# Taps summed by accumulating transposes, and the first layer's sums of two blocks split from their PSUM banks

## The chip, the cores and the metric

One core of a Trainium2 chip runs the kernel. The metric is the device time of one execution in microseconds (us), median of several runs. The profile comes from one execution of its own; its span is the part between its first and its last recorded instruction.

## The reference

```python
# attention: x is (2, 4096, 192); weight_gen is (2, 4096, 8 heads, 7 taps)
w = softmax(weight_gen over the 7 taps)
out[b, s, h, g] = sum over k of w[b, s, h, k] * x_pad[b, s + k, h, g]     # causal window of 7
# two dense layers over the 8192 tokens, d_model 192, d_ff 2048
h = x @ w_in1;  x = (h * cos(h)) @ w_out1
h = x @ w_in2;  return maximum(0.01 * h, h) @ w_out2
```

The kernel gets the four weight matrices as 64-bit floats, seen as pairs of 32-bit integers.

## The kernel before

**Blocks and chunks.** The 8192 tokens are 16 blocks of 512 (four groups of 128), taken in the order `LINE` = 2, 3, 0, 1, 4, 5, ... A block passes through attention, layer 0 and layer 1. A layer runs over 16 chunks of 128 hidden units. `hidden` (L707) makes one chunk's `h` (128 x 512) in a PSUM bank with five matmuls. After it ACT makes the turns of the angle `g` (L719), DVE the angle (L726), ACT the sine (L731), DVE the product (L736), and the result is split into `hi` and `lo` (a rounded part and the remainder, fp32r). Two projections add it up over the chunks in two banks `accm` and `accr`: `project_hi` with three matmuls (L763 to L765) and `project_lo` with two (L768, L769). So a chunk costs ten matmuls of 512 columns.

**192 = 128 + 64.** Of the 192 features, 128 are the main part (`tm`, `x0hi`, `x0lo`, `ihi`, `ilo`, `am`), 64 the rest (`tr`, `x0rh`, `x0rl`, `r`, `ar`). The rest's `hi` and `lo` weights are stacked on the 128 partitions of `r` by four DMAs (L661) from `whi` and `wlo`. So the fourth matmul of a chunk waits for those DMAs.

**Attention.** For blocks 2 and 3 (`SUMMED`), DVE multiplies each tap (L503, 128 x 768, three row buffers `pr`), and PE adds the seven taps up in the banks `tm` and `tr` by matmuls against the identity, which transposes as well (L508). The other 14 blocks add the taps on DVE and transpose once (L474, L479). The banks are then split: `x0hi` (ACT), `x0lo` (DVE), `x0rh` and `x0rl`.

**Weights.** Each layer's weights come in four groups, and each of these as an `in` and an `out` part. Loads into two `raw` buffers are followed by: size (ACT, L611), clamp (POOL, L614), shift (DVE, L619), merge (DVE, L625), low (ACT, L633), add (POOL, L638), then the split into hi (ACT) and lo (POOL). A `raw` buffer is free after merge and low. Only group (0, 0) is treated in two parts (main 512 columns, rest 256).

**Hand-over.** `take` copies a block's layer-0 sums out of the two banks (`om`, `sw`, `s`) and splits them into layer 1's `x1hi`, `x1lo`, `x1rh`, `x1rl`, the rest in halves (`place`).

**Order.** Nothing runs in a loop on the chip. A planner (`Plan.emit`) takes operations with due times and cost estimates and writes them out one by one; each engine, and the DMA queue SP, then works strictly in the order written. A `due` that changes, or a cost that changes, may move any later row. Names such as `pr_3_189` are tap 3 with a running number; `h_2_4` is chunk 4 of block 2.

Of the kernel before, what the change touches and what calls it, by code (L numbers as in the profile page):

```python
# [9 lines left out]
F32 = mybir.dt.float32  # L10
# [184 lines left out]
def conv_attention_moe_moe(ctx, tc, x, weight_gen, w_in1, w_out1, w_in2, w_out2, out):  # L195
# [68 lines left out]
    def minus(e, out, a, b):  # L264
        eng[e].tensor_tensor(out=out, in0=a, in1=b.bitcast(F32), op=ALU.subtract)  # L265
# [45 lines left out]
    def steps_of(t):  # L311
        return t()[:, : 2 * Q * CW].rearrange("p (s h k) -> p s h k", h=H, k=K)

    def softmax(s0, s1, due):
        n = s1 - s0
        w = temp([P, 16, H, K], "smw", 2, f"smw{s0}")
        m = temp([P, 16, H], "smm", 2, f"smm{s0}")
        k = ("smw", s0)
        part = n / 16
        early = s0 // Q in SUMMED  # L320
# [18 lines left out]
        op(due - 3, {"ACT": 0.2 + 0.8 * part + (2.6 if s0 // Q not in SUMMED else 0)}, lambda e: nc.scalar.activation(  # L339
            out=W(), in_=W(), func=AF.Exp), [k], [k], bufs)  # L340
# [15 lines left out]
    def x_load(b, due):  # L356
        t = Buf(lambda: xin.tile([P, (Q + HALO) * D], F32, tag="xt", name=f"xt{b}"), "xt", 2, line="xt")
        first = Q * b - HALO
        own = max(-first, 0)
        xt_of[b] = t, own  # L360

        def body(e, j0, j1):
            nc.sync.dma_start(out=t()[:, j0 * D : j1 * D], in_=xf[:, (first + j0) * D : (first + j1) * D])

        steps = [(HALO, Q + HALO), (own, HALO)] if b in SUMMED else [(own, Q + HALO)]
# [119 lines left out]
    def attention_summed(b, begins):  # L485

        xt, own = xt_of[b]
        ksm, smw, s0 = sm_of[b]
        tm, tr = bank(f"tm{b}", ("tq", 2)), bank(f"tr{b}", ("tq", 2))
        x_tiles(0, b)  # L490
        last = begins - 2
        for i, k in enumerate(reversed(range(K))):
            pr = row(f"pr{b}_{k}")
            reads = [ksm, ("xt", b, 1)]
            if k < HALO:
                reads.append(("xt", b, 2))
            if k < own:
                reads += [("xt", b, 0, *j) for j in ((0,), (1,), ("z", 0), ("z", 1))]

            def product(e, k=k, pr=pr):  # L500
                win = xt().rearrange("p (q h g) -> p q h g", h=H, g=G)[:, k : k + Q]
                wgt = steps_of(smw)[:, s0 : s0 + Q][:, :, :, k].unsqueeze(3).to_broadcast([P, Q, H, G])
                eng[e].tensor_tensor(out=pr().rearrange("p q (h g) -> p q h g", h=H), in0=win, in1=wgt, op=ALU.mult)  # L503

            def total(e, to, c, i=i, pr=pr):
                for q in range(Q):
                    v = pr()[:, q, c]
                    nc.tensor.matmul(  # L508
                        to()[: v.shape[-1], q * P : (q + 1) * P], v, ident,
                        start=i == 0 and q == 0, stop=i == K - 1 and q == Q - 1,  # L510
                    )

            due = last - (K - i) * PACE[b]
            op(due, {"DVE": 1.0}, product, reads, [("pr", b, k)], [xt, smw, pr])
            for to, key, c, late in ((tm, "tm", slice(0, P), 0.5), (tr, "tr", slice(P, D), 0.55)):
                op(due + late, {"PE": 0.58}, lambda e, to=to, c=c, total=total: total(e, to, c),
                   [("pr", b, k), "ident"] + ([(key, b)] if i else []), [(key, b)], [pr, to])
        turned(b, last, tm, tr)

# [37 lines left out]
    def weights(m, g):  # L557
# [9 lines left out]
        def load(raw):  # L567
            nc.sync.dma_start(out=raw()[:, : GF * P].rearrange("p c w -> p (c w)"), in_=wi[:P, c2])
# [10 lines left out]
            )  # L579

        U = 3 * half
        for i in ("in", "out"):
            due = need[m, g * GF] + {"in": -0.6, "out": 1.8}[i]
            raw = temp([P, U, 2], "raw", 2, f"w{n}{i}", I32)
# [1 line left out]
            v = temp([P, U], "wn", 2, f"wn{n}{i}", I32)  # L586
            if i == "in":
                parts = [(0, GF * P), (GF * P, U)]
                op(due - 6, {"SP": 1.75}, lambda e, raw=raw: load(raw), (), [("raw", n, i, 0)], [raw])
                for j in range(2):  # L590
                    op(due - 6, {"SP": 0.4}, lambda e, raw=raw, j=j: load_rest(raw, j), (), [("raw", n, i, 1, j)], [raw])
                loaded = [[("raw", n, i, 0)], [("raw", n, i, 1, 0), ("raw", n, i, 1, 1)]]
# [100 lines left out]
    def chunk(pos, st, m, b, f):  # L693
# [177 lines left out]
```

## Time and profile before

| | |
|---|---|
| three runs, median (lowest to highest) | 1248.27 us (1247.76 to 1248.58) |
| the profiled execution's own time | 1247.06 us |
| its span | 1245.2 us |
| PE busy | 1222.1 us |
| DVE, ACT, POOL busy | 890.6, 850.6, 448.0 us |

An engine's busy time is the time covered by its records. PE's matmuls overlap in the records (one of 512 columns is recorded as 0.39 us, but the next starts 0.23 us later), so for PE the distance from start to start counts.

### The profile page before, as it was taken

How to read it: one execution, taken by the hardware profiler on the slowest of the kernel's cores; microseconds unless marked ns; L12 is line 12 of the kernel's file. 1: busy time of each engine (PE TensorE's matmuls, PEld its weight loads, DVE VectorE, ACT ScalarE, POOL GpSimd, SP SyncE). 2: the span in 40 equal slices, each digit the busy share in tenths (PEclk: the TensorE clock that was granted, in tenths of full speed). 3: DMA queues.
4: the chain of work that ended last, by engine and by line, in shares of the span. 5: the costliest groups of instructions: out<-in, count | busy, mean ns of one | idle time of the engine just before them, and what ended most of it. 6: DMA issues, size and time to landing. Idle time of an engine off the chain costs nothing.

```text
span 1245.2 us, 15437 instructions
## 1 busy us (share of the span) xinstructions
PE 1222.1 (98%) x5524; PEld 1002.6 (81%) x5524; DVE 890.6 (72%) x1364; ACT 850.6 (68%) x1552; POOL 448.0 (36%) x340
## 2 busy tenths in 40 slices
PE   7999899999999999999999999999999999999998
PEld 6777687788888888888888888888888888888886
DVE  6799899889676777757677686777768676655433
ACT  4798766788675777667676767767667576655654
POOL 3686632566232323323233233323324232322000
PEclk9999999999999999999999999999999999999999
DMA  5343410100001010010101001010000100000000
GB/s 181 91 127 93 132 41 13 45 33 1 1 1 60 1 45 1 1 45 1 46 1 60 1 1 45 1 45 1 25 21 1 46 1 13 1 1 13 1 13 26
DMA packets 15469, 39.51 MB, mean 32 GB/s; under 512 B 1828, under 2 KB 8482, under 8 KB 15392
## 3 DMA queue, kind: packets, MB, share of 16 engines
q1 hardware_dynamic: 15392, 38.53, 9.6%
q8 instruction: 43, 0.70, 0.2%
q14 instruction: 34, 0.28, 0.1%
HBM read 30.13 MB, written 6.29 MB: 29 GB/s over the span
## 4 chain that ended last, share of the span: by engine, by line
PE 91%; DVE 4%; ACT 2%; DMA 1%; issue 1%; SPq 0%; POOL 0%; DVEq 0%; ACTq 0%; POOLq 0%
PE h L707 44%; PE acc0r L768 4%; PE acc0m L763 4%; PE acc1m L763 4%; PE acc1r L768 4%; PE acc1m L769 4%; PE acc1r L765 4%; PE acc1m L764 4%; PE acc0r L765 4%; PE acc0m L769 4%; PE acc0m L764 4%; PE tm L508 1%; PE tr L508 1%; DVE g L726 1%; PE pm L809 1%
## 5 line engine op out<-in xcount | busy, mean ns | idle before, releaser
L265 POOL TENSOR_TENSOR lo<-g,hi 128x512 fp32r<-128x512 f32 x240 | 340.1, 1418 | 606.3 <-ACT hi L260 497.0
L726 DVE SCALAR_TENSOR_TENSOR g<-g,h 128x512 f32<-128x512 int32 x256 | 174.9, 685 | 165.5 <-ACT g L719 163.9
L265 DVE TENSOR_TENSOR lo<-h,hi 128x512 fp32r<-128x512 f32 x272 | 186.4, 687 | 94.3 <-ACT hi L260 92.4
L719 ACT ACTIVATE g<-h 128x512 int32<-128x512 f32 x238 | 141.4, 594 | 137.5 <-PE h L707 136.7
L750 ACT ACTIVATE h<-h 128x512 f32<-128x512 f32 x256 | 148.9, 582 | 84.1 <-PE h L707 83.1
L731 ACT ACTIVATE g<-g 128x512 f32<-128x512 f32 x256 | 160.6, 629 | 58.0 <-DVE g L726 57.3
L736 DVE TENSOR_TENSOR g<-h,g 128x512 f32<-128x512 f32 x240 | 164.6, 686 | 36.1 <-ACT g L731 31.1
L260 ACT ACTIVATE hi<-g 128x512 fp32r<-128x512 f32 x238 | 149.5, 629 | 47.6 <-DVE g L736 46.1
L260 ACT ACTIVATE hi<-h 128x512 fp32r<-128x512 f32 x225 | 133.6, 594 | 9.1 <-POOL lo L265 0.4
L763 PE MATMUL acc1m<-hi,ohi 128*128 128x512 f32 x256 | 102.3, 400 | 2.3 <-DVE hi L262 1.3
L707 PE MATMUL h<-x0hi,ihi 128*128 128x512 f32 x256 | 100.6, 393 | 3.2 <-DVE lo L265 1.4
L763 PE MATMUL acc0m<-hi,ohi 128*128 128x512 f32 x256 | 101.6, 397 | 2.1 <-DVE hi L262 1.1
L768 PE MATMUL acc0r<-lo,or 128*128 128x512 f32 x256 | 100.5, 393 | 1.2 <-DVE lo L265 0.8
L707 PE MATMUL h<-x0rh,r 128*128 128x512 f32 x256 | 99.7, 390 | 1.2 <-DMA r<-wlo 1.2
L707 PE MATMUL h<-x1hi,ihi 128*128 128x512 f32 x256 | 100.9, 394 | 0.0
L707 PE MATMUL h<-x1rh,r 128*128 128x512 f32 x256 | 99.9, 390 | 0.9 <-DMA r<-wlo 0.9
L768 PE MATMUL acc1r<-lo,or 128*128 128x512 f32 x256 | 100.1, 391 | 0.2
L707 PE MATMUL h<-x0rl,r 128*128 128x512 f32 x256 | 99.8, 390 | 0.1
L765 PE MATMUL acc0r<-hi,or 128*128 128x512 f32 x256 | 99.9, 390 | 0.0
L707 PE MATMUL h<-x1rl,r 128*128 128x512 f32 x256 | 99.8, 390 | 0.0
L769 PE MATMUL acc0m<-lo,ohi 128*128 128x512 f32 x256 | 99.8, 390 | 0.0
L765 PE MATMUL acc1r<-hi,or 128*128 128x512 f32 x256 | 99.8, 390 | 0.0
(248 smaller groups left out, 2466.1 us busy)
## 6 DMA issues: line engine op xcount, KB each, us to landing
xt<-in_x SPq DMA_DIRECT2D x12, 960.0 KB, 5.0
out<-osb SPq DMA_DIRECT2D x16, 384.0 KB, 2.6
smw<-in_weight_gen SPq DMA_DIRECT2D x3, 448.0 KB, 6.3
xt<-in_x SPq DMA_DIRECT2D x3, 384.0 KB, 5.3
xt<-in_x SPq DMA_DIRECT2D x2, 576.0 KB
r<-whi SPq DMA_DIRECT2D x16, 64.0 KB, 4.6
r<-wlo SPq DMA_DIRECT2D x16, 64.0 KB, 3.5
w00out<-in_moe_w_out SPq DMA_DIRECT2D x2, 384.0 KB, 7.7
```

Source lines behind the costliest of these rows:

```text
L260: nc.scalar.activation(out=out, in_=in_, func=AF.Copy)
L265: eng[e].tensor_tensor(out=out, in0=a, in1=b.bitcast(F32), op=ALU.subtract)
L707: nc.tensor.matmul(h(), w[:, c], v(), start=i == 0, stop=i == len(terms) - 1)
L719: nc.scalar.activation(out=k, in_=h(), func=AF.Copy, scale=0.5 / math.pi, bias=0.25)
L726: nc.vector.scalar_tensor_tensor(out=g(), in0=g().bitcast(I32), scalar=-2 * math.pi, in1=h(), op0=ALU.mult, op1=ALU.add)
L731: nc.scalar.activation(out=g(), in_=g(), func=AF.Sin, bias=math.pi / 2)
L736: nc.vector.tensor_tensor(out=h() if bank_low else g(), in0=h(), in1=g(), op=ALU.mult)
L750: op(pos + 0.6, {"ACT": 0.58}, lambda e: nc.scalar.activation(out=h(), in_=h(), func=AF.Prelu, alpha=0.01), [kh], [kg], [h])
L763: nc.tensor.matmul(am(), ohi[:, f % GF, :], ghi(), start=first, stop=False)
L765: nc.tensor.matmul(ar(), orr[:, f % GF, :], ghi(), start=first, stop=False)
L768: nc.tensor.matmul(ar(), orr[:, f % GF, :], glo(), start=False, stop=last)
L769: nc.tensor.matmul(am(), ohi[:, f % GF, :], glo(), start=False, stop=last)
```

## The change

1. In `total` the matmuls against the identity become transposes (`is_transpose=True`) that accumulate in the same banks; the planner's cost for four goes from 0.58 to 0.44.
2. For blocks 2 and 3 a new `hand_over` takes the place of `take`: `x1hi` and `x1lo` are made straight from the bank `am`, and the rest is summed and split over 512 columns at once.
3. Group (0, 0): the rest part of the `in` weights is due 2.5 earlier. All groups: `whi`, `wlo` and the four `r` DMAs are due 0.5 to 1 earlier.
4. The main load of group (0, 1) is written behind the four `r` DMAs of group (0, 0) (`first_rest`).

The other edits rename conditions and leave the same blocks chosen.

```diff
+    DIRECT = set(LINE[:2])
...
                 for q in range(Q):
                     v = pr()[:, q, c]
                     nc.tensor.matmul(
-                        to()[: v.shape[-1], q * P : (q + 1) * P], v, ident,
+                        to()[: v.shape[-1], q * P : (q + 1) * P], v, ident, is_transpose=True,
                         start=i == 0 and q == 0, stop=i == K - 1 and q == Q - 1,
                     )
...
-            op(due, {"DVE": 1.0}, product, reads, [("pr", b, k)], [xt, smw, pr])
+            op(due, {"DVE": 0.95 if smw is sm_bank else (0.95,)}, product, reads, [("pr", b, k)], [xt, smw, pr])
...
+        first_rest = [(("00", "r"), p, j) for p in ("hi", "lo") for j in range(2)]
...
-                op(due - 6, {"SP": 1.75}, lambda e, raw=raw: load(raw), (), [("raw", n, i, 0)], [raw])
+                op(due - 6, {"SP": 1.75}, lambda e, raw=raw: load(raw), first_rest if (m, g) == (0, 1) else (), [("raw", n, i, 0)], [raw])
...
+                due = need[m, g * GF] + {"in": -0.6, "out": 1.8}[i] - (2.5 if i == "in" and pn else 0)
...
-                op(due - 4, {"ACT": 0.42, "DVE": (0.29,)}, lambda e, hi=hi, t=t: copy(e, hi(), t().bitcast(F32)[:, rest]), kts[-1:], [(n, "whi")], [t, hi])
+                op(due - 4.5, {"ACT": 0.42, "DVE": (0.29,)}, lambda e, hi=hi, t=t: copy(e, hi(), t().bitcast(F32)[:, rest]), kts[-1:], [(n, "whi")], [t, hi])
...
+    def hand_over(due, b, am, ar):
+
+        hi, lo, rh, rl = x_tiles(1, b)
+        sw = temp([P, T], "om", 2, f"sw{b}")
+        s = temp([P, T], "om", 2, f"s{b}")
+        k = [("acc", 0, b)]
+        up, dn = slice(0, R), slice(R, P)
+        op(due, {"ACT": 0.58}, lambda e: copy(e, sw()[up], ar()[dn]), k, [("sw", b)], [ar, sw])
+        op(due + 0.1, {"ACT": 0.58, "DVE": 0.67}, lambda e: copy(e, hi(), am()), k, [("xhi", 1, b)], [am, hi])
+        op(due + 0.2, {"DVE": 0.68}, lambda e: nc.vector.tensor_tensor(out=s()[up], in0=ar()[up], in1=sw()[up], op=ALU.add),
+           k + [("sw", b)], [("s1", b)], [ar, sw, s])
+        op(due + 0.3, {"DVE": 0.67}, lambda e: minus(e, lo(), am(), hi()), k + [("xhi", 1, b)], [("xlo", 1, b)], [am, hi, lo])
+        due = min(due + 4, begin[1, b] - 2.5)
+        whole = ("s1", b)
+        op(due, {"ACT": 0.62, "DVE": (0.43,)}, lambda e: copy(e, rh()[up], s()[up]), [whole], [("rh", 1, b, 0)], [rh, s])
+        op(due + 0.3, {"DVE": (0.675,), "POOL": 1.28}, lambda e: minus(e, rl()[up], s()[up], rh()[up]),
+           [whole, ("rh", 1, b, 0)], [("rl", 1, b, 0)], [rh, rl, s])
+        op(due + 0.4, {"ACT": 0.62, "DVE": (0.43,)}, lambda e: copy(e, rh()[dn], s()[up]), [whole], [("rh", 1, b, 1)], [rh, s])
+        op(due + 0.6, {"DVE": (0.43,), "ACT": 0.63}, lambda e: copy(e, rl()[dn], rl()[up].bitcast(F32)), [("rl", 1, b, 0)], [("rl", 1, b, 1)], [rl])
...
         am, ar = acc_of[st]
+        if m == 0 and b in DIRECT:
+            return hand_over(due, b, am, ar)
```

The order of the engines moves at three places that matter below. First SP's queue, from the load of block 3's `xt` on, before:

```order
L363 DMA xt_169<-in_x 128x1152
L568 DMA w01in<-in_moe_w_in 128x1024
L572 DMA w01in<-in_moe_w_in 64x512
L661 DMA r_80<-whi_251 64x256 x2
L572 DMA w01in<-in_moe_w_in 64x512
L661 DMA r_80<-wlo_268 64x256 x2
L576 DMA w01out<-in_moe_w_out 128x2x384 x2
```

The same place now:

```order
L364 DMA xt_174<-in_x 128x1152
L665 DMA r_80<-whi_240 64x256 x2
L665 DMA r_80<-wlo_251 64x256 x2
L573 DMA w01in<-in_moe_w_in 64x512 x2
L569 DMA w01in<-in_moe_w_in 128x1024
L577 DMA w01out<-in_moe_w_out 128x2x384 x2
```

The four `r` DMAs of the first group moved ahead of all three loads of `w01in`, which now come in the order rest, rest, main.

Second PE, from the end of block 2's chunk 1 to its first projection (`acc0m`), before:

```order
L707 MATMUL h_2_1_309<-x0rl_282,r_80 128x512
L508 MATMUL tm_322<-ident,pr_6_304 128x128 x4
L508 MATMUL tr_331<-ident,pr_6_304 64x128 x4
...
L508 MATMUL tm_322<-ident,pr_3_354 128x128 x4
L707 MATMUL h_2_2_373<-x0hi_271,ihi_78 128x512
...
L508 MATMUL tr_331<-ident,pr_3_354 64x128 x4
L763 MATMUL acc0m_391<-hi_380,ohi_81 128x512
```

The same place now:

```order
L711 MATMUL h_2_1_306<-x0rl_282,r_80 128x512
L711 MATMUL h_2_2_319<-x0hi_265,ihi_78 128x512
...
L509 MATMUL tm_330<-ident,pr_6_303 128x128 x4
L509 MATMUL tm_330<-ident,pr_5_315 128x128 x4
L509 MATMUL tm_330<-ident,pr_4_325 128x128 x4
L509 MATMUL tr_360<-ident,pr_6_303 64x128 x4
...
L767 MATMUL acc0m_382<-hi_371,ohi_81 128x512
```

Chunk 2 comes right behind chunk 1, and block 3's tap 3 moved behind the first projection.

Third ACT, from block 2's `x0rl` to the first `hi` of a chunk, before:

```order
L260 ACTIVATE x0rl_282<-x0rl_282 64x512
L611 ACTIVATE wt01in<-w01in 128x768
L633 ACTIVATE wn01in<-w01in 128x768
L260 ACTIVATE ohi_81<-wt00out 128x256 x2
L260 ACTIVATE or_83<-wt00out 128x2x64 x2
L719 ACTIVATE g_319<-h_2_0_296 128x512
L719 ACTIVATE g_329<-h_2_1_309 128x512
L731 ACT_TABLE_LOAD
L731 ACTIVATE g_319<-g_319 128x512
L611 ACTIVATE wt01out<-w01out 128x768
L731 ACTIVATE g_329<-g_329 128x512
...
L260 ACTIVATE hi_380<-g_319 128x512
```

The same place now:

```order
L261 ACTIVATE or_83<-wt00out 128x2x64
L614 ACTIVATE wt01in<-w01in 128x768
L636 ACTIVATE wn01in<-w01in 128x768
L723 ACTIVATE g_328<-h_2_0_290 128x512
L723 ACTIVATE g_336<-h_2_1_306 128x512
L723 ACTIVATE g_347<-h_2_2_319 128x512
L735 ACT_TABLE_LOAD
L735 ACTIVATE g_328<-g_328 128x512
L614 ACTIVATE wt01out<-w01out 128x768
L735 ACTIVATE g_336<-g_336 128x512
L261 ACTIVATE hi_371<-g_328 128x512
```

The four splits of `wt00out` moved ahead of the two passes over `w01in`, a third chunk's turns came in, and the first `hi` stands one pass earlier; the turns stay behind `w01in`.

## Rows read from the trace of the kernel before

**Rows 1.** The page: its first line, and busy time of two engines.

```profile
span 1245.2 us, 15437 instructions
PE 1222.1 (98%) x5524; PEld 1002.6 (81%) x5524; DVE 890.6 (72%) x1364; ACT 850.6 (68%) x1552; POOL 448.0 (36%) x340
```

**Rows 2.** Busy time by stretch: PE, PEld, DVE, ACT, POOL, then PEclk (granted clock).

```profile
5.00:10.00 5.00, 3.36 (x15) 3.17 (x16) 3.53 (x6) 0.56 (x2) 0.57 (x1) 1.00 0.96 255
...
50.00:60.00 10.00, 9.67 (x43) 7.48 (x42) 8.54 (x13) 9.32 (x17) 6.72 (x6) 1.00 0.18 49
...
110.00:120.00 10.00, 7.49 (x30) 5.11 (x29) 9.72 (x15) 7.91 (x15) 5.50 (x6) 1.00 0.13 39
120.00:130.00 10.00, 8.04 (x34) 5.62 (x32) 9.31 (x13) 8.40 (x15) 9.59 (x8) 1.00 0.56 147
```

**Rows 3.** Busy time by stretch at the very end, behind the last matmul.

```profile
1242.00:1246.00 4.00, 0.00 (x0) 0.00 (x0) 0.00 (x0) 0.00 (x0) 0.00 (x0) 0.61 0.25 98
```

**Rows 4.** The chain that ended last: start, length, what.

```profile
6.64 2.05 PE tm L508 x8
...
12.73 1.09 PE tm L508 x8
13.82 1.03 PE tr L508 x8
...
19.55 5.55 DMA w01in<-in_moe_w_in
```

**Rows 5.** Timeline of PE (start, length, line, output<-inputs): six transposes of another block.

```profile
180.17 0.60 PE L474 MATMUL tm<-ident,xa 128*128 128x128 f32 x4
180.60 0.38 PE L479 MATMUL tr<-ident,xb 128*128 128x128 f32 x2
```

**Rows 6.** Timeline of all engines, block 2's taps and the first weights.

```profile
7.09 1.81 DVE L503 TENSOR_TENSOR pr<-xt,smb 128x768 f32<-128x768 f32 x2
...
11.50 0.40 POOL L614 TENSOR_SCALAR wt00in<-wt00in 128x256 f32<-128x256 f32 x1 [0.30 <-ACT wt00in L611]
...
16.29 1.02 DVE L625 SCALAR_TENSOR_TENSOR wt00in<-w00in,wt00in 128x512 int32<-128x512 int32 x2
...
17.54 0.40 ACT L260 ACTIVATE whi<-wt00in 128x256 fp32r<-128x256 f32 x1
...
18.27 1.23 SPq L661 DMA_DIRECT2D r<-whi  x2
...
19.20 0.73 POOL L265 TENSOR_TENSOR wlo<-wn00in,whi 128x256 fp32r<-128x256 f32 x1
...
25.89 0.91 ACT L611 ACTIVATE wt01in<-w01in 128x768 f32<-128x768 f32 x1
...
28.52 1.05 ACT L719 ACTIVATE g<-h 128x512 int32<-128x512 f32 x2
```

**Rows 7.** DMA issues: operations, KB each, median us to landing.

```profile
w03in<-in_moe_w_in SPq DMA_DIRECT2D x1, 512.0 KB, 4.9
...
w02in<-in_moe_w_in SPq DMA_DIRECT2D x2, 128.0 KB, 4.2
```

**Rows 8.** Timeline of all engines, block 2's first chunks.

```profile
33.56 0.62 ACT L260 ACTIVATE hi<-g 128x512 fp32r<-128x512 f32 x1
...
34.06 0.96 DVE L625 SCALAR_TENSOR_TENSOR wt01in<-w01in,wt01in 128x768 int32<-128x768 int32 x1
...
37.68 0.50 PE L763 MATMUL acc0m<-hi,ohi 128*128 128x512 f32 x1
...
42.82 0.89 ACT L611 ACTIVATE wt02in<-w02in 128x768 f32<-128x768 f32 x1 [0.25 <-DMA w02in<-in_moe_w_in]
...
48.15 0.50 PE L707 MATMUL h<-x0hi,ihi 128*128 128x512 f32 x1
...
54.40 0.39 PE L763 MATMUL acc0m<-hi,ohi 128*128 128x512 f32 x1
```

**Rows 9.** Timeline of all engines, block 2's hand-over.

```profile
109.62 1.86 DVE L265 TENSOR_TENSOR x1rl<-s,x1rh 64x256 fp32r<-64x256 f32 x2
```

More of the change, by code (lines that the diff above doesn't have):

```diff
@@ L319, in softmax @@
         part = n / 16
-        early = s0 // Q in SUMMED
+        early = s0 // Q in LINE[:2]
         for b in range(s0 // Q, s1 // Q):
@@ L338, in softmax @@
         op(due - 4, {"DVE": (0.16 + 0.925 * part,), "POOL": 0.18 + 1.59 * part}, lambda e: wide(e, ALU.subtract), [k], [k], bufs)
-        op(due - 3, {"ACT": 0.2 + 0.8 * part + (2.6 if s0 // Q not in SUMMED else 0)}, lambda e: nc.scalar.activation(
+        op(due - 3, {"ACT": 0.2 + 0.8 * part + (2.6 if s0 // Q not in LINE[:2] else 0)}, lambda e: nc.scalar.activation(
             out=W(), in_=W(), func=AF.Exp), [k], [k], bufs)
@@ L363, in body @@
             nc.sync.dma_start(out=t()[:, j0 * D : j1 * D], in_=xf[:, (first + j0) * D : (first + j1) * D])
-        steps = [(HALO, Q + HALO), (own, HALO)] if b in SUMMED else [(own, Q + HALO)]
+        steps = [(HALO, Q + HALO), (own, HALO)] if b in LINE[:2] else [(own, Q + HALO)]
         for i, (j0, j1) in enumerate(steps):
@@ L494, in attention_summed @@
             reads = [ksm, ("xt", b, 1)]
-            if k < HALO:
+            if k < HALO and b in LINE[:2]:
                 reads.append(("xt", b, 2))
@@ L501, in product @@
                 win = xt().rearrange("p (q h g) -> p q h g", h=H, g=G)[:, k : k + Q]
-                wgt = steps_of(smw)[:, s0 : s0 + Q][:, :, :, k].unsqueeze(3).to_broadcast([P, Q, H, G])
+                wgt = (steps_of(smw) if smw is sm_bank else smw())[:, s0 : s0 + Q][:, :, :, k].unsqueeze(3).to_broadcast([P, Q, H, G])
                 eng[e].tensor_tensor(out=pr().rearrange("p q (h g) -> p q h g", h=H), in0=win, in1=wgt, op=ALU.mult)
@@ L508, in total @@
                     nc.tensor.matmul(
-                        to()[: v.shape[-1], q * P : (q + 1) * P], v, ident,
+                        to()[: v.shape[-1], q * P : (q + 1) * P], v, ident, is_transpose=True,
                         start=i == 0 and q == 0, stop=i == K - 1 and q == Q - 1,
                     )
-            due = last - (K - i) * PACE[b]
-            op(due, {"DVE": 1.0}, product, reads, [("pr", b, k)], [xt, smw, pr])
+            due = last - (K - i) * PACE.get(b, 2.6)
+            op(due, {"DVE": 0.95 if smw is sm_bank else (0.95,)}, product, reads, [("pr", b, k)], [xt, smw, pr])
             for to, key, c, late in ((tm, "tm", slice(0, P), 0.5), (tr, "tr", slice(P, D), 0.55)):
-                op(due + late, {"PE": 0.58}, lambda e, to=to, c=c, total=total: total(e, to, c),
+                op(due + late, {"PE": 0.44}, lambda e, to=to, c=c, total=total: total(e, to, c),
                    [("pr", b, k), "ident"] + ([(key, b)] if i else []), [(key, b)], [pr, to])
@@ L648, in weights @@
             kts, kvs = [d[0] for d in done], [d[1] for d in done]
+            due = need[m, g * GF] + {"in": -0.6, "out": 1.8}[i]
             if i == "in":
@@ L653, in weights @@
                 rest = slice(GF * P, U)
-                op(due - 4, {"ACT": 0.42, "DVE": (0.29,)}, lambda e, hi=hi, t=t: copy(e, hi(), t().bitcast(F32)[:, rest]), kts[-1:], [(n, "whi")], [t, hi])
-                op(due - 3.3, {"POOL": 0.73}, lambda e, hi=hi, lo=lo, v=v: minus(e, lo(), v().bitcast(F32)[:, rest], hi()),
+                op(due - 4.5, {"ACT": 0.42, "DVE": (0.29,)}, lambda e, hi=hi, t=t: copy(e, hi(), t().bitcast(F32)[:, rest]), kts[-1:], [(n, "whi")], [t, hi])
+                op(due - 4.3, {"POOL": 0.73}, lambda e, hi=hi, lo=lo, v=v: minus(e, lo(), v().bitcast(F32)[:, rest], hi()),
                    [*kvs[-1:], (n, "whi")], [(n, "wlo")], [v, hi, lo])
@@ L660, in weights @@
                     for name, src, rows in (("hi", hi, slice(0, R)), ("lo", lo, slice(R, P))):
-                        op(due - 3, {"SP": 0.4}, lambda e, src=src, rows=rows, c=c, r=r: nc.sync.dma_start(
+                        op(due - 4, {"SP": 0.4}, lambda e, src=src, rows=rows, c=c, r=r: nc.sync.dma_start(
                             out=ir[rows, c].bitcast(F32), in_=src()[r].bitcast(F32)), [(n, f"w{name}")], [((n, "r"), name, j)], [src])
@@ L777, in chunk @@
             take(pos + 3, st, m, b)
+    def hand_over(due, b, am, ar):
[16 more added lines that the diff above has]
+        op(due + 0.6, {"DVE": (0.43,), "ACT": 0.63}, lambda e: copy(e, rl()[dn], rl()[up].bitcast(F32)), [("rl", 1, b, 0)], [("rl", 1, b, 1)], [rl])
+        for i in ("rh", "rl"):
+            for j in (2, 3):
+                plan.writers[i, 1, b, j] = plan.writers[i, 1, b, 1]
     def take(due, st, m, b):
         am, ar = acc_of[st]
+        if m == 0 and b in DIRECT:
+            return hand_over(due, b, am, ar)
         n = f"{m}_{b}"
```

## The prediction

> **What bounds the kernel now.** Read the page first: PE is busy for 1222.1 of 1245.2 us [rows 1], so 23.1 us are idle, 6.64 of them before the first tap [rows 4]. The busy time by stretch then says where PE waits: it loses 2.51 us in 110 to 120 and 1.96 in 120 to 130, where DVE is busy for 97% and 93% [rows 2]. Whatever PE saves ahead of the long full stretch moves the end, if the head of the program can run that much earlier. The timeline of the head decides that, and there PE is not the only limit: around 50 us ACT is busy 93% and DVE 85% of the time [rows 2].
>
> **PE's work.** The only PE work that changes is the taps of blocks 2 and 3: 7 taps x 2 blocks, each a `tm` and a `tr` group. A group is recorded as eight passes and takes 1.09 and 1.03 us [rows 4]: 14 x 2.12 = 29.7 us. What four accumulating transposes cost is not in the trace; the nearest rows are four plain transposes, whose successor starts 0.43 us later [rows 5]. I take 0.43 (start-to-start) for both kinds, as the operands are the same: 28 x 0.43 = 12.0. So 17.7 us of PE work go. The other bound is that accumulation keeps the old 1.09 and nothing goes. The Trainium skill (TensorE: Matmul & The Clock Gate, Terms) gives fp32 transposes as four times faster than the matmul; by it four would take 0.27 us and 22 us would go. The rows say 2.5 times, and the row is taken.
>
> **How much of it the head keeps.** I walk the new order with old durations.
>
> *Block 2's taps.* Two products take 1.81 us, the third tap's ends at 8.9 [rows 6]. DVE then no longer waits for PE to release a row buffer (a tap costs PE 0.86, DVE 0.95) and does taps 3 and 2 until 10.9. The rest part's shift, now ahead of tap 1, waits for POOL's clamp, which ends at 11.6 to 11.9 (11.9 before, with one ACT pass more in front) [rows 6]. Then tap 1, the rest's merge (0.42 of the 1.02), the main shift and tap 0: rest's merge done at 13.25, tap 0 at 14.6, the main merge at 15.8, the transposes at 15.5. Before, PE set the pace: 14.85 + four more taps at 2.12 = 23.3.
>
> *The r DMAs and w01in.* `whi` ends at 13.65 (0.40), POOL's add and `wlo` (0.73) at 14.8, so SP issues four r DMAs (0.6 each) by 16.0, two rest loads of `w01in` by 17.2 and its main load by 17.6. Landing takes 4.9 us (a main load [rows 7]) to 5.55 (`w01in` itself [rows 4]): 22.2 to 23.1, against 25.1 before. The moved r DMAs, with no load in front, land by about 20.
>
> *Chunks 0 to 2.* `ihi` follows the merge and `x0hi` on ACT, at 16.4. `ilo` takes two POOL passes of about 1.3 (`wlo` by width) behind the main merge, to 18.4; `x0rl` is there at 18.6 to 19.9. So chunk 0 ends by 20.4 and chunk 2 by 22.7. But their turns stand on ACT behind two passes over `w01in` (0.91 each [rows 6]). The first turn starts at 22.2 + 1.85 = 24.05, against 28.52 [rows 6]: **4.5 us** earlier, not 6.
>
> *First projection.* From the first turn to `hi` ACT took 33.56 - 28.52 = 5.04 us [rows 6, 8]. The third turn adds 0.6 and the low pass that moves behind takes 0.9 away; some gaps stay, so again 5.1: `hi` ends at 29.8. Before, PE came to the projection 3.5 us after `hi` was done (34.18 to 37.68 [rows 8]), because it was still adding taps. Now it waits for `hi` (idle from about 24.3), and projects at 29.85: 7.8 us ahead.
>
> *Chunk 4 of block 2.* Taps 3 to 0 of block 3 follow at 0.86 each. DVE's products hold PE back between them, and h of chunk 4 begins at 38.2, 10 us ahead of 48.15 [rows 8]. Here the weights catch up: `w01in`'s merge ends at 32.5 (35.0 before [rows 8]), so `w02in` is issued from 32.5, its rest loads by 35.3, and lands 4.2 us after the second issue [rows 7], at 39.0 to 39.5. ACT's pass over it stands ahead of chunk 3's `hi` and `x0hi` of block 3, and ACT is free at 37.7. So about 1.5 us of ACT time are lost on a wait that was 0.25 before [rows 8]. Behind it lie two half turns, two turns, two sines and the weights' splits; chunk 4's `hi` ends at 46.5, its projection starts at 46.6 against 54.40: **7.8 us** gained, 6.9 if `w01in` lands at 23.1. I take 7.3. The remaining 10 us of the 17.7 become PE's wait at 24 to 30 and around 45.
>
> From there on each engine has the work it had, in nearly the old order, so I let the gain stand until the hand-over.
>
> **Hand-over.** Per block it drops a DVE copy and two quarter-size casts, puts one 512-column operation in place of each pair, and takes `x1lo` off POOL onto DVE. What a 64 x 512 subtraction on DVE costs here is bounded by 0.6 (the products' 0.9 for 768 columns [rows 6], by width) and 1.86, which the two old halves took beside POOL [rows 9]. DVE's work stays about equal, but `x1hi` no longer waits for a copy. PE's waits in 110 to 130 sum to 4.5 us [rows 2]: from 4.5 gained to 2.5 lost (the 110 to 120 loss once more, from reordering). Earlier `whi`, `wlo` and r DMAs pull the same way. I take 1.5 gained.
>
> **The clock.** The profile gives a granted clock of 1.00 (the 2.4 GHz level) from 5 to 10 us [rows 2], yet the first `tm` group took 2.05 against 1.09 later [rows 4], as at 1.2 GHz. After the last matmul the granted clock of 4 us means 0.61 [rows 3], so it does fall when PE stops. The new head gives PE less to do and an idle stretch of 5 us at 24 to 30. If it ran at the lower level up to the first chunks, block 2's taps would end at 18.5 and chunk 2 at 26.5 instead of 22.7; only the third turn comes later than the others' wait for `w01in`, by 1.4 us. A second slow start at 30 costs up to 2. So 0 to 3.5 lost; I take 1.0.
>
> **Sum.** 7.3 + 1.5 - 1.0 = 7.8 us. The span goes to 1237.4 and this execution's own time from 1247.06 to 1239.3. The runs' median is 1.2 above that execution, so 1248.27 - 7.8 = **1240.5**.
>
> **The rivals.**
>
> *All of PE's work comes back.* If the waits at 24 to 46 are filled (loads land earlier than the rows say, DVE and ACT are early enough), the gain nears 17.7, at most 1248.3 - 17.7 = 1230.6. For it: PE is the page's bound. Against: first turns tied to `w01in`. 0.12.
>
> *The transposes don't get faster when they accumulate.* Then the taps end at 23 as before, the splits and ACT's row of work behind them too, and the turns come no earlier than the old 28.5: 1247, if the earlier r DMAs give 1. For it: no row shows an accumulating transpose. Against: the transpose rows have the same operands. 0.05.
>
> *The clock stays low through the head (slower).* The new head holds 25.7 us of PE work at the full clock up to 46.6 (28 groups x 0.43, eight chunks at 5 x 0.227, four projections at 5 x 0.227). If all of it ran at the lower level it would take 51.4, end at 58.0 instead of 54.4, and the kernel would take 3.6 more: 1252. It decides once the low level covers more than the 14 us of slack that the head has. Against: the old taps sped up within 6 us [rows 4]. The Trainium skill (TensorE: Matmul & The Clock Gate, Part 4: PE-mode transpose) says that the full clock doesn't engage for transposes; no row of before can show it, since its transposes stand between matmuls. By that rule the taps, not the 60 matmuls of the chunks and projections, run low. 0.06.
>
> *The new order costs in the second layer's start.* Two group loads and the hand-over share ACT, DVE and POOL at 104 to 130, and the planner wrote them anew. If a late `wt11in` or `x1rl` doubles the 4.5 us of waits and the clock takes 3.5, the gain falls to 7.3 - 4.5 - 3.5: 1248.9, no change. Milder forms give 1244 to 1247. 0.15.
>
> **Chances and range.** The forecast, 1237 to 1244, gets 0.62. A measurement here tells 0.2% (2.5 us) from no change, so faster means below 1245.8. Of the rival in the second layer's start 0.09 is faster, 0.04 the same and 0.02 slower; of the transposes 0.04 is the same, 0.01 faster; of the clock 0.05 slower, 0.01 the same. Sum: faster 0.62 + 0.12 + 0.09 + 0.01 = 0.84, same 0.09, slower 0.07. The range takes in most of the first rival and the mild form of the last: 1233.5 to 1246.5.
>
> **What the new profile would show.** PE's four-transpose groups 0.43 to 0.45 apart; chunk 0 done at about 20; ACT waiting for `w01in` at 21 to 22 and the first turn at 24; PE idle for 5 us before the first projection at 30; ACT waiting for `w02in` near 38; the first projection of chunk 4 at 46.6; 110 to 130, moved 7 us forward, with less than 4.5 us of waits; the stretch from 200 on without change but for the shift. I am wrong if the first turn comes before 22 or after 26, if transposes take more than 0.6 per four behind the first tap, or if the gain at chunk 4 is given back by 200 us.

## The result and the profile after

| | before | after |
|---|---|---|
| median of the runs (lowest to highest) | 1248.37 us (1247.76 to 1248.58, 4 runs) | 1236.96 us (1236.70 to 1237.60, 4 runs) |
| own time of the profiled execution | 1247.06 us | 1237.60 us |
| its span | 1245.2 us | 1235.8 us |
| PE busy | 1222.1 us | 1208.9 us |

The changed kernel takes 0.991 of the time (95% interval 0.9893 to 0.9927). The two profiled executions are 9.46 us apart, the medians 11.4, since the profiled one of before was faster than its timed runs and that of after the slowest of its four. In a second set of five runs (after_again) the changed kernel took 1237.52 us against 1247.17 (0.9922, 0.9908 to 0.9936). The steps below are compared span to span: 9.4 us.

The page of the changed kernel, the rows that answer to [rows 1]:

```profile
span 1235.8 us, 15183 instructions
PE 1208.9 (98%) x5412; PEld 991.9 (80%) x5412; DVE 886.1 (72%) x1358; ACT 848.5 (69%) x1546; POOL 447.3 (36%) x338
```

PE is busy 13.2 us less, not 17.7. Most of the difference is in the next view: busy time by stretch of the changed kernel (PE, PEld, DVE, ACT, POOL, then the granted clock).

```profile
15.00:20.00 5.00, 2.38 (x11) 1.71 (x12) 4.71 (x9) 2.18 (x4) 4.09 (x4) 0.88 0.47 112
20.00:25.00 5.00, 5.00 (x13) 3.58 (x12) 4.94 (x8) 4.05 (x9) 3.66 (x4) 0.50 0.77 254
25.00:30.00 5.00, 2.96 (x22) 2.42 (x22) 2.86 (x5) 4.61 (x7) 2.55 (x5) 0.94 0.00 1
50.00:60.00 10.00, 7.81 (x32) 5.53 (x31) 8.18 (x13) 8.07 (x16) 8.27 (x8) 1.00 0.58 149
110.00:120.00 10.00, 9.29 (x40) 6.90 (x38) 9.07 (x15) 8.24 (x14) 9.00 (x10) 1.00 0.75 240
120.00:130.00 10.00, 8.61 (x37) 6.79 (x37) 8.87 (x13) 9.46 (x17) 6.38 (x6) 1.00 0.45 123
```

From 20 to 25 the granted clock is 0.50, the 1.2 GHz level, so the same matmuls count for twice the busy time. In 110 to 130 PE idles 0.71 + 1.39 = 2.1 us, where it idled 4.5 [rows 2]; in 50 to 60 it idles 2.2, where it idled 0.3.

The timeline of the changed kernel, all engines (start, length, engine, line, output and inputs, idle time before it and what ended that), at the places that the prediction named:

```profile
7.63 1.06 PE L509 MATMUL tr<-ident,pr 128*64 128x128 f32 x4
...
8.49 1.06 PE L509 MATMUL tm<-ident,pr 128*128 128x128 f32 x4
...
12.37 0.60 PE L509 MATMUL tr<-ident,pr 128*64 128x128 f32 x4
12.81 0.60 PE L509 MATMUL tm<-ident,pr 128*128 128x128 f32 x4
...
16.97 0.50 PE L711 MATMUL h<-x0hi,ihi 128*128 128x512 f32 x1 [0.77 <-ACT ihi L261]
...
18.43 0.58 SPq L569 DMA_DIRECT2D w01in<-in_moe_w_in  x1
...
19.22 0.80 PE L711 MATMUL h<-x0hi,ilo 128*128 128x512 f32 x1 [1.75 <-POOL ilo L266]
...
22.70 0.92 ACT L614 ACTIVATE wt01in<-w01in 128x768 f32<-128x768 f32 x1 [0.90 <-DMA w01in<-in_moe_w_in]
...
24.37 1.05 ACT L723 ACTIVATE g<-h 128x512 int32<-128x512 f32 x2
...
25.79 0.60 ACT L723 ACTIVATE g<-h 128x512 int32<-128x512 f32 x1 [0.36 <-PE h L711]
...
29.10 1.50 PE L509 MATMUL tr<-ident,pr 128*64 128x128 f32 x12 [2.04 <-DVE g L740]
30.36 0.47 PE L767 MATMUL acc0m<-hi,ohi 128*128 128x512 f32 x1
...
32.69 0.96 DVE L628 SCALAR_TENSOR_TENSOR wt01in<-w01in,wt01in 128x768 int32<-128x768 int32 x1
...
40.75 0.91 ACT L614 ACTIVATE wt02in<-w02in 128x768 f32<-128x768 f32 x1 [2.44 <-DMA w02in<-in_moe_w_in]
...
47.59 0.39 PE L767 MATMUL acc0m<-hi,ohi 128*128 128x512 f32 x1
...
57.90 0.50 PE L767 MATMUL acc0m<-hi,ohi 128*128 128x512 f32 x1 [1.35 <-ACT hi L261]
...
61.44 0.39 PE L767 MATMUL acc0m<-hi,ohi 128*128 128x512 f32 x1
...
101.52 0.67 DVE L266 TENSOR_TENSOR x1lo<-acc0m,x1hi 128x512 fp32r<-128x512 f32 x1
...
103.57 0.68 DVE L266 TENSOR_TENSOR x1rl<-s,x1rh 64x512 fp32r<-64x512 f32 x1
```

From 12.37 on, groups of four transposes start 0.44 us apart. The first turn comes at 24.37, the first projection at 30.36, chunk 4's projection at 47.59. That last one was at 54.40 [rows 8], so 6.8 us are gained by then and 2.6 behind it. Those 2.6 are a loss and a larger gain: five projections later (61.44 above) the old kernel was at

```profile
65.75 0.39 PE L763 MATMUL acc0m<-hi,ohi 128*128 128x512 f32 x1
```

so the lead is down to 4.3 us there, and 5.1 come behind it.

### The profile page after: what moved, and what is told of

Same layout as the page of the kernel before. It is cut to its first block, busy times and chain, and to the rows that moved or that the text cites. A ratio compares the mean times of both kernels' runs of the same rounds, so it can differ in the third digit from the quotient of the medians.

```text
span 1235.8 us, 15183 instructions
## 1 busy us (share of the span) xinstructions
PE 1208.9 (98%) x5412; PEld 991.9 (80%) x5412; DVE 886.1 (72%) x1358; ACT 848.5 (69%) x1546; POOL 447.3 (36%) x338
## 4 chain that ended last, share of the span: by engine, by line
PE 88%; DVE 4%; ACT 4%; DMA 2%; issue 1%; SPq 1%; POOL 0%; ACTq 0%; DVEq 0%
PE h L711 44%; PE acc1m L767 5%; PE acc1m L773 4%; PE acc1r L772 4%; PE acc1r L769 4%; PE acc1m L768 4%; PE acc0m L767 4%; PE acc0r L769 4%; PE acc0m L768 4%; PE acc0r L772 4%; PE acc0m L773 4%; ACT hi L261 1%; DMA w00in<-in_moe_w_in 1%; DVE g L740 1%; DVE lo L266 1%
## 5 line engine op out<-in xcount | busy, mean ns | idle before, releaser
L711 PE MATMUL h<-x0hi,ilo 128*128 128x512 f32 x256 | 100.6, 393 | 1.7 <-POOL ilo L266 1.7
L711 PE MATMUL h<-x0lo,ihi 128*128 128x512 f32 x256 | 100.4, 392 | 0.0
```

Source lines behind the costliest of these rows:

```text
L711: nc.tensor.matmul(h(), w[:, c], v(), start=i == 0, stop=i == len(terms) - 1)
```

## The experiments

Each ratio is to the kernel before, run on the same chip (its medians were 1247.2 to 1247.8).

### Which part brings it

**t_only**: the kernel before with the transposes. The planner's cost for four of them is 0.44 here too; with it the order stays as it was, but for one projection (three matmuls on PE at 40 us).

```diff
-                        to()[: v.shape[-1], q * P : (q + 1) * P], v, ident,
+                        to()[: v.shape[-1], q * P : (q + 1) * P], v, ident, is_transpose=True,
...
-                op(due + late, {"PE": 0.58}, lambda e, to=to, c=c, total=total: total(e, to, c),
+                op(due + late, {"PE": 0.44}, lambda e, to=to, c=c, total=total: total(e, to, c),
```

> The order of before, word for word, with the taps of blocks 2 and 3 as accumulating transposes; nothing else. Head-chain theory (the gain is an earlier first turn on ACT, tied to the landing of w01in, and PE no longer late at the first projection): the two passes over w01in start at 22 to 23, but the four splits of wt00out still stand ahead of the turns, so the first turn comes at about 26 (28.5 before, 24.4 with the whole change), the first projection at 31 to 32 (37.7 before). Time 1242 to 1244. Rival, PE work alone counts: 1248.4 - 17.7 = 1231. Rival, the new order alone counts: 1247 to 1248.

Measured: 1238.62 us, 0.9929 (0.9917 to 0.9942). The expectation missed: without the other edits the transposes bring some 9 us. It had put the passes over `w01in` at 22 to 23 and the first turn at 26. They came at 21.08, earlier than in the changed kernel, since the main load of `w01in` still stands ahead of the `r` DMAs, and at 23.76 (timeline of t_only, all engines; the last row is chunk 4's projection, 2.1 us ahead of the changed kernel's):

```profile
21.08 0.92 ACT L611 ACTIVATE wt01in<-w01in 128x768 f32<-128x768 f32 x1 [2.10 <-DMA w01in<-in_moe_w_in]
...
45.45 0.50 PE L763 MATMUL acc0m<-hi,ohi 128*128 128x512 f32 x1 [1.48 <-ACT hi L260]
```

**no_t**: the changed kernel in its own order, with plain matmuls for the transposes.

```diff
-                        to()[: v.shape[-1], q * P : (q + 1) * P], v, ident, is_transpose=True,
+                        to()[: v.shape[-1], q * P : (q + 1) * P], v, ident,
```

> The order of the changed kernel, word for word, but the taps by plain matmuls as before. Head-chain theory: the taps again run until about 23 and the first projection waits behind three chunks and six tap groups on PE, at about 35; chunk 4 of block 2 is back near its old place (54), and only the hand-over's 2 to 3 us stay: 1244 to 1247. Rival, PE work alone counts: 1237 + 17.7 = 1255. Rival, the new order alone counts: 1237 to 1239.

Measured: 1246.13 us, 0.9986 (0.9977 to 0.9995), as expected. Order and hand-over without fast transposes are worth 1.6 us.

**no_direct**: the changed kernel with `take` for all blocks.

```diff
-    DIRECT = set(LINE[:2])
+    DIRECT = set()
```

> The changed kernel with the old take for blocks 2 and 3 in place of hand_over (the planner moves some rows behind it). Between the first projection of chunk 4 and the stretch from 200 on the changed kernel gained another 2.6 us on the old one. If the hand-over gave that, the time is 1238.5 to 1240; if it gave nothing (the r DMAs and the shifted weights did), 1236.5 to 1237.5.

Measured: 1240.48 us, 0.994 (0.9928 to 0.9953). The hand-over is worth 3 to 3.5 us in the changed kernel. Busy time of no_direct over its hand-over:

```profile
100.00:130.00 30.00, 27.39 (x109) 20.75 (x108) 25.37 (x45) 27.73 (x51) 20.19 (x17) 0.94 0.38 121
```

PE idles 2.6 us there (2.2 in the changed kernel), and the mean granted clock is 0.94: with 0.12 of the 30 us at half speed, (1 - 0.94) x 30 = 1.8 us more are lost. Behind it, from 130 to 200, PE idles 3.4 against 2.4.

**no_wts**: the changed kernel with the weights' dues and `first_rest` undone (the dues of `whi`, `wlo` and the `r` DMAs likewise).

```diff
-                op(due - 6, {"SP": 1.75}, lambda e, raw=raw: load(raw), first_rest if (m, g) == (0, 1) else (), [("raw", n, i, 0)], [raw])
+                op(due - 6, {"SP": 1.75}, lambda e, raw=raw: load(raw), (), [("raw", n, i, 0)], [raw])
...
-                due = need[m, g * GF] + {"in": -0.6, "out": 1.8}[i] - (2.5 if i == "in" and pn else 0)
+                due = need[m, g * GF] + {"in": -0.6, "out": 1.8}[i]
```

> The changed kernel with the old due times of all weights and without first_rest, so the main load of w01in stands ahead of the r DMAs again and whi behind ihi. Head-chain theory: w01in lands at about the same time (22 to 23), since taps and merge are as early, but the r DMAs land later and chunk 0 waits for them until about 22; turns within 1 us of the changed kernel's 24.4. Time 1237 to 1239.5. Rival, the weights' order carries the gain: 1241 or more.

Measured: 1238.29 us, 0.9926 (0.9912 to 0.9939). The weights' edits bring 0.8 to 1.3 in the changed order, at the edge of what these runs can tell.

**t_take**: t_only and `hand_over`, nothing else. So the planner's new cost for four transposes is in it, which its expectation leaves out; the old cost of a product is kept.

```diff
...
+        if m == 0 and b in SUMMED:
+            return hand_over(due, b, am, ar)
```

> The kernel before with transposes and with hand_over for blocks 2 and 3, and none of the other edits (dues of the weights, costs of taps). The two gains seen apart were 9 us (transposes alone in the old order, chunk 4's projection at 45.45 against 47.59) and 3 us (changed kernel with and without hand_over). If they add up, 1235.5 to 1236.5, ahead of the changed kernel, and the weights' dues cost. If the head's lead of 2.1 us is given back at a wait behind it, as in the kernel with transposes alone, 1236.5 to 1238.5, like the changed kernel without the weights' dues.

Measured: **1233.70 us, 0.9888 (0.9875 to 0.9902)**, faster than the changed kernel. So transposes and hand-over add up, to some 14 us, and the remaining edits (the weights' dues and the planner's estimate for a product) take 3 of them back.

### What binds the head

**few_taps**: the changed order; of block 3's seven taps PE adds two.

```diff
-                for q in range(Q):
+                for q in range(Q if b == LINE[0] or i in (0, K - 1) else 0):
```

> The order of the changed kernel, in which PE adds only the first and the last of block 3's seven taps (five tm and five tr groups are left out, so block 3's values are not the reference's). That takes 10 groups x 0.43 = 4.3 us of PE work out of the head, three of the pairs ahead of the first projection. If PE no longer binds the head (it waits about 14 us in its first 50), only the 1.3 us of tr groups in front of the first projection can matter, and of them 0.2, since hi is ready at 30.15 and the projection came at 30.36: 0 to 0.6 faster, 1236.4 to 1237.0. If PE's work still sets the head's end, most of 4.3 comes back: 1233 to 1234.

Measured: 1237.57 us, 0.9915 (0.9902 to 0.9929): no gain. At chunk 4 it was 1.3 ahead (46.33), and the granted clock of 50 to 60 was 0.83, which costs (1 - 0.83) x 10 = 1.7 us. So of 4.3 us of PE's work at most 1.3 reached chunk 4: in the main, PE's own work is no longer what binds the head.

**warm**: 17 idle matmuls on PE in front of the first tap, of chunk 0 and behind its first matmul.

```diff
...
+                if pos == 0 and i < 2:
+                    keep_busy((3, 6)[i])
                 nc.tensor.matmul(h(), w[:, c], v(), start=i == 0, stop=i == len(terms) - 1)
...
+            nc.tensor.matmul(spare[0][:, :P], ident, ident, start=True, stop=True)
```

> The changed kernel with 17 idle matmuls of 128 columns added on PE into a bank that nothing reads yet: 8 ahead of the first tap, 3 ahead of chunk 0 and 6 behind chunk 0's first matmul, where PE waited. They shall keep the granted clock at 1.00 through the first taps and chunks 0 to 2 (the first six tap groups were 0.85 apart instead of 0.43, and 20 to 25 had 0.50). If the low clock was covered by the wait for w01in, only the third turn's wait of 0.36 and its like can go: 0.2 to 0.8 faster, 1236.2 to 1236.8. If the slow stretch was paid in full (2.6 us in the taps, 2.8 in the chunks), 3 to 5 us faster: 1232 to 1234. If the added matmuls stand in the way, slower by as much as they overrun the wait, up to 1.

Measured: 1236.66 us, 0.9914 (0.9901 to 0.9928), no gain that can be told. That is what was expected of a low clock that is covered, but the run can't show it, since the low clock moved and did not go. Busy time by stretch of warm:

```profile
20.00:25.00 5.00, 4.32 (x22) 3.18 (x23) 4.67 (x7) 3.78 (x9) 3.76 (x4) 1.00 0.71 240
25.00:30.00 5.00, 1.76 (x10) 1.28 (x9) 2.82 (x5) 4.97 (x8) 2.83 (x6) 0.74 0.01 2
30.00:40.00 10.00, 10.00 (x55) 8.43 (x54) 8.01 (x12) 4.32 (x8) 6.28 (x5) 0.79 0.43 106
```

Chunks 0 to 2 now run at 1.00 and end 2.4 us earlier, and the first `hi` ends at 29.59 instead of 30.15. PE then waits 3.24 us in front of block 3's `tr` groups and falls to the lower level there instead: the first projection came at 30.97 and chunk 4's at 47.33, against 30.36 and 47.59. The changed kernel itself, run again (after_again), had part of the low stretch in either place:

```profile
20.00:25.00 5.00, 5.00 (x23) 3.84 (x22) 4.92 (x7) 4.00 (x9) 3.88 (x5) 0.77 0.71 238
...
30.00:35.00 5.00, 5.00 (x28) 4.17 (x27) 4.96 (x8) 2.55 (x6) 2.79 (x2) 0.75 0.22 33
```

In all three (1 - granted clock) x length comes to 3.4 us from 5 to 50, and the spans are 1234.9 to 1235.8. So the place of the low stretch doesn't show in the time. What it would be worth to be rid of it is not shown: no run with the fast transposes has a head without one.

### Which order costs

All the kernels here hold the same transposes; only rows move.

**merge_first**: in the changed kernel the merge of `w01in` waits for two of block 3's products on DVE. Here block 3's last four products wait for it.

```diff
...
+        last, behind = begins - 2, lambda o, b, i: (b == LINE[1] and i >= 3) and (merged['01', 'in', 0].next.append(o), setattr(o, 'deps', o.deps + 1))
...
```

> The changed kernel, with block 3's last four products held behind the merge of w01in on DVE. The merge ran at 32.7 though its input was ready at 24.5; it frees the buffer for w02in, for which ACT then waits 2.44 us at 38 to 41. If the weights' chain sets the head's end, w02in is issued 1.5 to 3 us earlier, that wait shrinks to under 1, and the kernel is 1 to 2.5 us faster: 1234.5 to 1236. If DVE's products or PE's taps set it, block 3's taps come later and nothing is gained or up to 2 us lost: 1237 to 1239.

Measured: 1236.90 us, 0.9913 (0.99 to 0.9927): no difference. Its timeline, all engines (the third row is chunk 4's projection):

```profile
31.10 0.96 DVE L628 SCALAR_TENSOR_TENSOR wt01in<-w01in,wt01in 128x768 int32<-128x768 int32 x1
...
38.90 0.92 ACT L614 ACTIVATE wt02in<-w02in 128x768 f32<-128x768 f32 x1 [1.91 <-DMA w02in<-in_moe_w_in]
...
45.80 0.39 PE L767 MATMUL acc0m<-hi,ohi 128*128 128x512 f32 x1
...
121.47 0.48 PE L711 MATMUL h<-x1rh,r 128*128 128x512 f32 x1 [1.75 <-DMA r<-wlo]
...
122.04 0.63 PE L767 MATMUL acc1m<-hi,ohi 128*128 128x512 f32 x1
122.47 0.63 PE L768 MATMUL acc1m<-hi,olo 128*128 128x512 f32 x1
```

The head did what was asked: merge 1.6 earlier, chunk 4 1.8 earlier. But the moved rows put an `r` DMA of the second layer late (1.75 us), and behind that wait matmuls start 0.43 apart, at the lower level, for 3.4 us, which costs 1.7.

**turns_first**: ACT's two passes over `w01in` (`sized`, `lowed`) wait for the turns of chunks 0 and 1.

```diff
...
+    ahead = lambda o, pos: pos == 1 and [(o.next.append(v["01", "in", 0]), setattr(v["01", "in", 0], "deps", v["01", "in", 0].deps + 1)) for v in (sized, lowed)]
...
```

> The changed kernel with ACT's two passes over w01in held behind the turns of chunks 0 and 1. If the wait for w01in sets the head's end through the first turns, these come at 22 to 23.6, the first projection 0.5 to 1 us earlier, and the kernel is about that much faster: 1236. If the chain of the weights (w01in merged, then w02in loaded, then ACT's pass over it) sets it, w01in's passes end 1 to 1.5 us later and chunk 4's projection with them, unless the merge comes earlier on DVE: 1237 to 1238.5. No difference beyond 0.5 either way means that neither alone sets it.

Measured: 1238.65 us, 0.9928 (0.9915 to 0.994), 1.1 above the changed kernel beside it, with intervals that overlap. The first turn came at 21.50 (24.37), the first projection at 29.54, chunk 4's at 45.70. That lead is gone by 62, to a wait and the pace behind it (the tenth projection comes at 61.86, against 61.44); timeline of PE in turns_first:

```profile
56.72 0.50 PE L767 MATMUL acc0m<-hi,ohi 128*128 128x512 f32 x1 [1.86 <-ACT hi L261]
...
57.81 0.63 PE L767 MATMUL acc0m<-hi,ohi 128*128 128x512 f32 x1
58.24 0.63 PE L768 MATMUL acc0m<-hi,olo 128*128 128x512 f32 x1
```

**old_cost**: the changed kernel with the planner's old estimates for a tap.

```diff
-            op(due, {"DVE": 0.95 if smw is sm_bank else (0.95,)}, product, reads, [("pr", b, k)], [xt, smw, pr])
+            op(due, {"DVE": 1.0}, product, reads, [("pr", b, k)], [xt, smw, pr])
...
-                op(due + late, {"PE": 0.44}, lambda e, to=to, c=c, total=total: total(e, to, c),
+                op(due + late, {"PE": 0.58}, lambda e, to=to, c=c, total=total: total(e, to, c),
```

> The changed kernel with the planner's old estimates for the taps (0.58 for four transposes, 1.0 for a product), which moves rows and nothing else: the third chunk comes behind the first of block 3's taps again and the merge of w01in ahead of two products. The kernel with transposes and hand_over alone ran at 0.9888 of the time before and the changed one at 0.991. If the new estimates are what costs the difference, this one goes to 1232 to 1235. If the weights' dues and the place of w01in's load cost it, it stays at 1236 to 1239.

Measured: 1234.09 us, 0.9893 (0.988 to 0.9907), like t_take, and 3.4 us under the changed kernel on the same chip. The weights' dues don't cost; the order that follows from the two new estimates does (pe_cost, below, tells which). Its timeline, all engines, the same three places:

```profile
29.25 0.96 DVE L628 SCALAR_TENSOR_TENSOR wt01in<-w01in,wt01in 128x768 int32<-128x768 int32 x1
...
37.19 0.92 ACT L614 ACTIVATE wt02in<-w02in 128x768 f32<-128x768 f32 x1 [1.47 <-DMA w02in<-in_moe_w_in]
...
44.81 0.50 PE L767 MATMUL acc0m<-hi,ohi 128*128 128x512 f32 x1 [1.21 <-ACT hi L261]
```

**after_again**: the changed kernel, without an edit, beside old_cost and turns_first.

> The changed kernel itself, on the same chip as the two beside it, so that differences of 2 to 4 us need no detour over the kernel before: 1236 to 1238.

Measured: 1237.52 us, 0.9922 (0.9908 to 0.9936).

**pe_cost**: only the estimate of PE put back; DVE's stays at 0.95.

```diff
-                op(due + late, {"PE": 0.44}, lambda e, to=to, c=c, total=total: total(e, to, c),
+                op(due + late, {"PE": 0.58}, lambda e, to=to, c=c, total=total: total(e, to, c),
```

> The changed kernel with only one of the planner's two estimates put back (0.58 for four transposes; a product stays at 0.95). The planner then writes a third order: the first two chunks' turns go to DVE ahead of block 3's products, so they no longer stand behind ACT's passes over w01in, and the merge of w01in stands behind three of the products, at about 32.5 as in the changed kernel. By these rows the first hi comes near 28 and the first projection near 28.5, 1.9 us earlier. If the first turns set the head's end, 1.5 to 2 us faster than the changed kernel: 1235 to 1236. If the merge of w01in and the w02in load behind it set it, no gain: 1236.5 to 1238.5. If the estimate for the transposes alone made the difference between 1237 and 1234, it comes at 1233 to 1235.

Measured: 1239.65 us, 0.994 (0.9926 to 0.9953), slower than the changed kernel, which no theory had expected. From old_cost it differs in one number, the cost of a product (0.95 for 1.0), and that is worth 5.6 us; the new cost of four transposes, the difference to the changed kernel, gives 2.1 to 2.7 of them back. The changed kernel with the new cost of the transposes alone was not run. Timeline of pe_cost, all engines (first projection, merge, ACT's pass, chunk 4's projection):

```profile
28.01 0.59 PE L767 MATMUL acc0m<-hi,ohi 128*128 128x512 f32 x1 [1.80 <-ACT hi L261]
...
31.37 0.94 DVE L628 SCALAR_TENSOR_TENSOR wt01in<-w01in,wt01in 128x768 int32<-128x768 int32 x1
...
39.68 0.90 ACT L614 ACTIVATE wt02in<-w02in 128x768 f32<-128x768 f32 x1 [4.44 <-DMA w02in<-in_moe_w_in]
...
48.13 0.39 PE L767 MATMUL acc0m<-hi,ohi 128*128 128x512 f32 x1
```

The first projection is 2.35 us earlier than in the changed kernel and chunk 4's is no earlier (48.13 against 47.59, and 46.99 in after_again): the first turns don't set the head's end.

**The eight orders side by side.** The first three columns are starts in the timelines. PE's idle time from 50 to 400 is 350 less its busy time there; "low clock" is (1 - granted clock) x length, over the stretches behind 50 where it was under 1.00. The sum of columns 3 to 5 less that of the changed kernel stands beside the spans' difference. The last row is the changed kernel once more: two executions of one program are up to 0.7 us apart in the first three columns, so smaller differences say nothing.

| kernel | merge of `w01in` | ACT over `w02in` | chunk 4 projects | PE idle, 50 to 400 | low clock | sum, less after's | span, less after's |
|---|---|---|---|---|---|---|---|
| old_cost | 29.25 | 37.19 | 44.81 | 7.4 | 1.7 | -1.6 | -3.0 |
| t_take | 29.84 | 37.53 | 45.16 | 6.4 | 0 | -4.0 | -5.0 |
| t_only | 29.85 | 37.82 | 45.45 | 10.4 | 0 | +0.4 | +1.6 |
| no_wts | 30.71 | 38.98 | 46.52 | 9.3 | 1.7 | +2.0 | +1.5 |
| turns_first | 31.01 | 38.88 | 45.70 | 9.0 | 1.7 | +0.9 | +1.6 |
| merge_first | 31.10 | 38.90 | 45.80 | 7.1 | 1.7 | -0.9 | -1.0 |
| pe_cost | 31.37 | 39.68 | 48.13 | 9.2 | 1.7 | +3.5 | +3.0 |
| after | 32.69 | 40.75 | 47.59 | 7.9 | 0 | 0 | 0 |
| after_again | 31.96 | 40.12 | 46.99 | 8.3 | 0 | -0.2 | -0.1 |

ACT's pass over `w02in` follows the merge of `w01in` by 7.7 to 8.3 us in every order (the load is issued when the merge has freed the buffer), and chunk 4 projects 6.8 to 8.5 behind it. The head's end moves with that merge, and merge_first, made to move it by 1.6, moved chunk 4 by 1.8 (0.9 and 1.2 against after_again). pe_cost falls out: its merge is 1.3 earlier than the changed kernel's and chunk 4 is not; ACT waits 4.44 us for `w02in` there. The low clock of the head is not what parts the orders: in t_take and t_only it takes the same 3.4 us as in the changed kernel, and their chunk 4 is 1.5 to 2.4 earlier than in either of its runs. What is gained there is kept only if the waits from 50 to 200 don't grow, and each order places these anew. The sum misses the spans by up to 1.4 us: idle time between chunk 4 and 50, and the other order of chunks, are not in it.

## Why the prediction was right

The median of 1236.96 lies in the range, just under the forecast's lower end of 1237 and 3.5 below 1240.5. Of these, 1.6 are in the terms (9.4 against 7.8 between the spans); the rest comes from which execution was profiled. The terms themselves are not all right: two of them missed in opposite ways, and the total is closer than they are.

**PE's work.** Groups of four accumulating transposes are 0.44 apart once PE runs at full clock, as taken from the plain ones [rows 5]; the first six were 0.85 to 0.88 apart, and the pace came up at 11.90 with nothing but transposes on PE since 6.75. So the transposes do reach the full clock, against the rule that the clock rival leaned on. That the transposes don't get faster when they accumulate is refuted; t_only and no_t show that they are the change.

**How much the head keeps.** The walk met nearly every event: ACT's pass over `w01in` at 22.70 (22.2 to 23.1), the first turn at 24.37 (24.05), the first projection at 30.36 (29.85), the wait for `w02in` of 2.44 (about 1.5), chunk 4 at 47.59 (46.6): 6.8 us gained against 7.3. The pass at 22.70 is in part luck: the main load of `w01in` was issued only at 18.43, where the walk had 17.2 to 17.6 (its 22.2 counts from the one, its 23.1 from the other), and landed in 4.1 us, where it had 4.9 to 5.55. Two things were not in it: the `tr` groups of block 3 wait 2.04 us for a bank that chunk 0's product frees, and chunk 2 ends at 25.5 instead of 22.7, at the low clock. The first costs 0.2 (`hi` ends at 30.15), the second 0.36 on ACT (the third turn's wait). That the first turns stand behind `w01in` was true and beside the point: turns_first and pe_cost took them out and gained nothing. The tie that counts is the later one, merge, `w02in`, ACT; the prediction had it in its walk (32.5, 39 to 39.5) and walked right for that reason.

**All of PE's work comes back.** It did not: the whole gain is 11.4 us where 17.7 of PE's work go, t_only gives the transposes 9.1 of it, and in few_taps 4.3 us less of PE's work gained nothing. But 11.4 is no limit either: t_take, with the same transposes in another order, gained 14.1.

**Hand-over.** The term was too small: 1.5, where 5.1 came behind 61.44, and the runs put the hand-over itself at 3 to 3.5 (no_direct, of which 1.8 is a stretch at the lower level) and 4.9 (t_take against t_only). The 64 x 512 subtraction took 0.68 us, near the lower bound of 0.6, where the halves had taken 1.86 [rows 9]. Idle time fell by 2.3 us in 100 to 130 and by 1.3 in 130 to 200.

**"In nearly the old order, so I let the gain stand."** This step failed: in 50 to 60 PE idles 2.2 us instead of 0.3, 1.9 of it waiting for `hi` of ACT, and the lead falls from 6.8 to 4.3. It stayed unseen in the total since the hand-over's larger gain covers it. old_cost idles 0.4 there; it is 3.4 us faster in all, with a chunk 4 that is 2.8 earlier.

**The clock.** I took 1.0 off. It did fall, to 0.50 for some 6 us, but little of that is passed on: chunks 0 and 1 end at 23.4, ahead of the first turn at 24.37, which stands behind `w01in`, and the third turn waits 0.36 for chunk 2. A cost beyond that is not shown, since no run is free of it. That it stays low through the head, and that the second layer's start gets dearer (1249.0 by that rival's sum, not 1248.9), did not come about. The terms come to 6.8 - 2.5 + 5.1 = 9.4, the clock's cost included, where 7.3 + 1.5 - 1.0 = 7.8 had been taken.

## What to carry to other kernels

When PE's work ahead of a full stretch shrinks, walk the chain of the other engines to the first point at which all of them are full; what counts is the last resource that a late load waits for, here a staging buffer that a merge on DVE frees 8 us before ACT can go on. A planner's estimate that is nearer the truth doesn't make the order better: two estimates corrected by 0.05 and 0.14 us cost 3.4 us here, and the smaller correction is the one that cost (pe_cost against old_cost), so a change should be timed with the order that it had before as well. A lead gained in the head has to be followed through every later wait: of merge_first's 1.8 us at chunk 4 nothing that can be told was left in the time.

## What was not expected of the hardware

PE's clock did not come up with the first work. In the changed kernel the first six groups of transposes were 0.85 to 0.88 apart, until 11.9, although the granted clock of 5 to 15 is given as 1.00; in warm, PE had worked from 1.4 to 5.2 on idle matmuls and the first groups were 0.85 apart all the same, until 10.0.

In the full stretches the lower level could follow a single wait: after 1.75 us (merge_first at 121) and 1.86 us (turns_first at 57) matmuls of 512 columns were 0.43 apart instead of 0.23. After 1.35 us in the changed kernel (57.90), and after 2.04 us (29.10), with transposes behind it, the pace did not change; in after_again, the same program, the wait at that place was 2.99 us and the pace fell, until 32.4. What decides it stays open. In the two full stretches (1 - granted clock) x length came to 1.7 us, about as much again as the wait.
